# The MLP's Relu and square written to a row in SBUF instead of back into the PSUM bank, in units 0 to 4

## The chip, the cores and the metric

One core of a Trainium2 chip runs the kernel. The metric is the time of one execution on the device in microseconds (us); of several runs the median is taken.

Five engines work side by side, each through its own list of instructions in order: PE (TensorE, matmuls; its weight loads are listed apart as PEld), DVE (VectorE), ACT (ScalarE), POOL (GpSimd) and SP (SyncE, which here only issues DMAs). An engine that meets an instruction whose inputs are not ready waits there, and everything behind it in its list waits too. Matmuls write into PSUM, here in banks of 128 partitions by 512 f32 values; the other engines work on PSUM and on SBUF.

## The reference

Two rounds, each of a long convolution and an MLP, on 2048 tokens (S) of width D = 1024, hidden width F = 3584, all f32:

```python
def _A_ref(q, k, v, shift_k, ssm_k, ssm_D):
    for t in range(ks):                      # ks = 4, causal
        k_shift = k_shift + k_pad[:, t:t + S, :] * shift_k[:, ks - 1 - t][None, None, :]
    kv = k_shift * v
...                                          # long convolution along S by FFT
    y = y + kv * ssm_D[None, None, :]
    return q * y

def _B_ref(x, w1, b1, w2, b2):
    h = jnp.einsum("bsd,df->bsf", x, w1) + b1
    r = jnp.where(h > zero, h, zero)
    h = r * r
    return jnp.einsum("bsf,fd->bsd", h, w2) + b2

x = A_q
x = x + _A_ref(_layernorm(x), A_k, A_v, A_shift_k, A_ssm_k, A_ssm_D)
x = x + _B_ref(_layernorm(x), B_w1, B_b1, B_w2, B_b2)
x = x + _A_ref(_layernorm(x), A_k, A_v, A_shift_k, A_ssm_k, A_ssm_D)
x = x + _B_ref(_layernorm(x), B_w1, B_b1, B_w2, B_b2)
```

The change lies in `h = r * r` of the MLP.

## The kernel before

**Products.** Every f32 operand of a matmul is split into a high half `hi` (a cast to the PE's format fp32r) and a low half `lo = x - hi`. A product is then three matmuls, hi·hi, hi·lo and lo·hi, issued by `mm3` (lines 333 to 336).

**Units.** The MLP runs in eight units, one per layer and block of 512 tokens, in the order of line 35. Units 0 to 4 take the plain path, with which the change deals; units 5, 6 and 7 have a path of their own (`relu_w`, line 1540), in which Relu and square already go to a row in SBUF. Beside the units' matmuls, and woven into them step by step, run the convolution of the blocks to come, the normalization and the additions of results.

**A plain unit** has four chunks of seven hidden tiles of 128. For each hidden tile there are two steps "m1" of 12 matmuls each: they fill one bank [128 x 512] with W1·x. Then come the chunk's 14 steps "m2" (two halves of the output width by seven hidden tiles, 12 matmuls each), which multiply the results, `rh` and `rl`, by W2. The first hidden tile of the next chunk is put between the two halves. Unit 0 is followed by the unit of layer 1 on the same block; its last chunk runs "m2" on half of the tokens at a time, and at its end the first m1 steps of unit 1 are done ahead, some of them in other banks.

**Banks.** An m1 tile takes its bank from `ps1` (line 305), which has two in turn; the four of `ps2` hold the outputs, and two named `pt` belong to the convolution and are passed around by hand with `take` and `give` (lines 314 to 331). Line 1802 picks the bank, and only tiles done ahead on a `pt` bank are returned with `give`. A bank of `ps1` comes free by itself when its last reader has run; the matmul that wants it waits for that.

**Between m1 and m2** stands `relu2` (lines 1483 to 1494). Lines 1813 and 1814 schedule its first part (`k == 0`, on ACT: Relu with bias, square, cast to `rh`) one step after the tile's last m1 step, and its second part (`k == 1`, on DVE: the subtraction that gives `rl`) two steps after it. `lag` is a list of such delayed calls. The instructions then stand in their engines' lists behind whatever was issued before.

**The weights** are streamed from DRAM through a ring of `RAWS = 8` rows in SBUF, `wr`, of 128 x 512 f32 each. `row()` (line 971) takes a row; `drop` (line 978) marks it as read; `room()` (line 968) allows a load when the row eight places back was dropped at least two steps ago. `w_load` (line 982) issues the load on SP up to 8 steps ahead of the weight's use (lines 993, 995, 998), `w_hi` (line 1000) the cast on ACT up to 4 steps ahead (line 1006, into `whl`), `w_lo` (line 1009) the subtraction up to 3 ahead (line 1014, on DVE but for a part of unit 0's last chunk), and with it the row is dropped. `w_advance` (line 1024) calls them at each step. If the ring is full of rows that aren't dropped, `row()` issues the pending casts and subtractions earlier. Some split weights are stored by line 1022 and fetched ready-made later by line 1004, with no row.

**The convolution** issues work on all engines between the steps: line 354 and on for the data (364 and 366 on DVE, 411 the stores), line 428 and on for the filters (482 and 483 on DVE, 492 the stores), line 624 the loads of factors, line 524 the products on POOL, 528 their sums on DVE, 605 the stores of results.

Of the kernel before, what the change touches and what calls it, by code (L numbers as in the profile page):

```python
# [10 lines left out]
F32 = mybir.dt.float32  # L11
F32R = mybir.dt.float32r
AF = mybir.ActivationFunctionType
# [226 lines left out]
def tile_h3_mlp(ctx: ExitStack, tc: tile.TileContext, q, kT, vT, shk, ssmT, ssmD, w1, b1, w2, b2,  # L240
                fwd_t, pro_t, inv_t, sgn_t, out):
    nc = tc.nc
    V, A, G, PE, SY = nc.vector, nc.scalar, nc.gpsimd, nc.tensor, nc.sync
# [85 lines left out]
    def give(*tiles):  # L329
        for o in tiles:  # L330
            held[slot.pop(id(o))[0]] = False
# [639 lines left out]
    def row():  # L971
        while len(ring) >= RAWS and "freed" not in ring[-RAWS]:
            w_hi() if ptr["lo"] == ptr["hi"] else w_lo()
        x = {"t": mw.tile([P, 512], F32, name="wr", bufs=RAWS)}
        ring.append(x)
        return x

    def drop(*xs):
        for x in xs:
            x["freed"] = now[0]  # L980
# [19 lines left out]
    def w_hi():  # L1000
        n = ptr["hi"]
        t = his[n] = mw.tile([P, 2, 512], F32R, name="whl", bufs=6)
        if from_pair(n):
            SY.dma_start(t.bitcast(F32), WD[wsrc[n]])
        else:
            A.copy(t[:, 0], raws[n]["t"])  # L1006
        ptr["hi"] += 1

    def w_lo():
        n = ptr["lo"]  # L1010
        t = wts[n] = his.pop(n)
        if not from_pair(n):
            e = WLO.get(phase[0], "V")
            ENG[e[n % len(e)]].tensor_sub(t[:, 1], raws[n]["t"], t[:, 0].bitcast(F32))  # L1014
            drop(raws.pop(n))
        ptr["lo"] += 1
# [462 lines left out]
    b1t = ml.tile([P, FT], F32, name="b1t", bufs=1)  # L1479
# [1 line left out]
    lag = slag  # L1481

    def relu2(st, k):
        o = st["o"]
        if k == 0:
            A.activation(o, o, AF.Relu, bias=b1t[:, st["f"]:st["f"] + 1])  # L1486
            A.activation(o, o, AF.Square)
            st["hi"] = ml.tile([P, T], F32R, name="rh", bufs=FC + 1)
            A.copy(st["hi"], o)  # L1489
        else:  # L1490
            st["lo"] = ml.tile([P, T], F32R, name="rl", bufs=FC + 1)
            V.tensor_sub(st["lo"], o, st["hi"].bitcast(F32))  # L1492
            if st["give"]:
                give(o)

    def make_t():
        parts = [(p, dq) for p in range(FT // 2) for dq in range(2)]
# [269 lines left out]
    for s, (k, u, c, a, i, tts, w) in enumerate(steps):  # L1767
# [27 lines left out]
        if k == "m1":  # L1795
# [8 lines left out]
            o = rs[c, a]["o"]  # L1804
            for kk in range(4):
                t = slice(kk * P, (kk + 1) * P)
                mm3(o[:, t0:t1], wh[:, t], wl[:, t], xh[:, 4 * i + kk, t0:t1], xl[:, 4 * i + kk, t0:t1],
                    i == 0 and kk == 0, i == 1 and kk == 3)
            if i == 1 and u in WINO:
                for kk in range(4 if rs[c, a]["f"] % 2 else 2):  # L1810
                    lag.at(1 + kk, relu_w, rs[c, a], kk, rp)
            elif i == 1 and tts[-1] == NT - 1:
                lag.at(1, relu2, rs[c, a], 0)
                lag.at(2, relu2, rs[c, a], 1)
        elif k == "w2":
# [6 lines left out]
            hi, lo = rp[i][a]  # L1822
            for n in range(2):
                t = slice(n * P, (n + 1) * P)
# [11 lines left out]
        else:  # L1836
            if i == 0:
                os = {tt: ps2() for tt in tts}
            r = rs[c, i]
            for tt in tts:  # L1840
                t = slice(tt * P, (tt + 1) * P)
# [124 lines left out]
```

## Time and profile before

| | us |
|---|---|
| runs | 2754.60, 2755.72, 2758.86 |
| median | 2755.72 |
| profiled execution, first to last instruction | 2756.1 |
| granted PE clock, mean | 0.992 of full |
| PE busy / idle in it | 2694.2 / 61.9 |
| moved by DMA | 756.88 MB, 275 GB/s |

The profiled execution is one more run of the same program, taken by the hardware's profiler; its own time is its span. The chain of work that ended last is traced back from the last instruction, with shares of the span by engine:

```profile
PE 86%; DVE 6%; DMA 5%; issue 1%; ACT 1%; SPq 1%; POOL 0%; DVEq 0%; ACTq 0%; POOLq 0%
```

An engine's "busy" is the time in which one of its instructions ran; in a wait's row, "p <- DVE rl" is read as: PE's matmul into bank p waited for DVE's instruction that wrote rl. SPq is SP's list of DMA issues.

### The profile page before, as it was taken

How to read it: one execution, taken by the hardware profiler on the slowest of the kernel's cores; microseconds unless marked ns; L12 is line 12 of the kernel's file. 1: busy time of each engine (PE TensorE's matmuls, PEld its weight loads, DVE VectorE, ACT ScalarE, POOL GpSimd, SP SyncE). 2: the span in 40 equal slices, each digit the busy share in tenths (PEclk: the TensorE clock that was granted, in tenths of full speed). 3: DMA queues.
4: the chain of work that ended last, by engine and by line, in shares of the span. 5: the costliest groups of instructions: out<-in, count | busy, mean ns of one | idle time of the engine just before them, and what ended most of it. 6: DMA issues, size and time to landing. Idle time of an engine off the chain costs nothing.

```text
span 2756.1 us, 36563 instructions
## 1 busy us (share of the span) xinstructions
PE 2694.2 (98%) x12601; PEld 2237.7 (81%) x12601; DVE 1935.9 (70%) x3068; ACT 1110.9 (40%) x1937; POOL 826.3 (30%) x531
## 2 busy tenths in 40 slices
PE   7999899899999999999999999999999999999999
PEld 7888787887788888888788888888788788888887
DVE  7878797677787677778676655376787666664555
ACT  4354344433434333342233422244355454444443
POOL 2345564244542645326454265000100010001000
PEclk9999999999999999999999999999999999999999
DMA  8889898589988898788887877688898766676555
GB/s 260 267 298 321 281 311 287 199 302 351 305 294 308 305 330 294 272 303 302 317 286 259 310 270 286 217 290 292 303 308 274 289 229 214 226 275 204 176 164 202
DMA packets 378057, 756.88 MB, mean 275 GB/s; under 512 B 43904, under 2 KB 159248, under 8 KB 377872
## 3 DMA queue, kind: packets, MB, share of 16 engines
q1 hardware_dynamic: 377872, 754.55, 79.8%
q8 instruction: 99, 1.62, 0.2%
q14 instruction: 86, 0.70, 0.1%
HBM read 604.46 MB, written 149.95 MB: 274 GB/s over the span
## 4 chain that ended last, share of the span: by engine, by line
PE 86%; DVE 6%; DMA 5%; issue 1%; ACT 1%; SPq 1%; POOL 0%; DVEq 0%; ACTq 0%; POOLq 0%
PE p L334 26%; PE p L335 26%; PE p L336 26%; PE p L1089 2%; DMA wr<-w 1%; PE pt L336 1%; PE pt L335 1%; PE pt L334 1%; DVE whl L1014 1%; DMA whl<-wd_m 1%; DMA wd_m<-whl 0%; PE pt L594 0%; PE p L788 0%; DVE sm L528 0%; DMA cg<-gd 0%
## 5 line engine op out<-in xcount | busy, mean ns | idle before, releaser
L334 PE MATMUL p<-xh,whl 128*128 128x512 f32 (+1 forms) x1840 | 710.3, 386 | 20.2 <-DVE rl L1492 19.0
L524 POOL TENSOR_TENSOR cp<-cx,cg 128x384 f32<-128x384 f32 (+5 forms) x288 | 534.0, 1867 | 617.7 <-DVE sm L528 397.7
L336 PE MATMUL p<-xh,whl 128*128 128x512 f32 (+1 forms) x1840 | 705.9, 384 | 0.0
L335 PE MATMUL p<-xl,whl 128*128 128x512 f32 (+1 forms) x1840 | 705.5, 383 | 0.1
L1006 ACT CAST whl<-wr 128x512 fp32r<-128x512 f32 x638 | 385.9, 622 | 450.1 <-PE p L336 274.8
L334 PE MATMUL p<-whl,rh 128*128 128x512 f32 x1372 | 547.8, 399 | 1.8 <-DMA whl<-wd_m 1.7
L335 PE MATMUL p<-whl,rh 128*128 128x512 f32 x1372 | 543.0, 396 | 4.9 <-DVE whl L1014 4.9
L1014 DVE TENSOR_TENSOR whl<-wr,whl 128x512 fp32r<-128x512 f32 x624 | 489.4, 805 | 76.9 <-ACT whl L1006 72.1
L336 PE MATMUL p<-whl,rl 128*128 128x512 f32 x1372 | 542.3, 395 | 0.0
L334 PEld LDWEIGHTS p<-xh,whl 128*128 128x128 f32 x1840 | 347.7, 189 | 91.0 <-DVE rl L1492 11.9
L336 PEld LDWEIGHTS p<-xh,whl 128*128 128x128 f32 x1840 | 347.4, 189 | 68.2
L335 PEld LDWEIGHTS p<-xl,whl 128*128 128x128 f32 x1840 | 347.6, 189 | 66.5 <-DVE xl L1402 0.3
L335 PEld LDWEIGHTS p<-whl,rh 128*128 128x128 f32 x1372 | 259.4, 189 | 64.0 <-DVE whl L1014 6.4
L334 PEld LDWEIGHTS p<-whl,rh 128*128 128x128 f32 x1372 | 259.2, 189 | 62.2 <-DMA whl<-wd_m 4.0
L336 PEld LDWEIGHTS p<-whl,rl 128*128 128x128 f32 x1372 | 259.0, 189 | 60.7
L528 DVE TENSOR_REDUCE sm<-cp 128x128 f32<-128x384 f32 (+5 forms) x288 | 249.8, 875 | 13.2 <-POOL cp L524 11.4
L1590 POOL TENSOR_TENSOR acc<-acc,px 128x512 f32<-128x512 f32 x18 | 23.1, 1318 | 770.3 <-DMA px<-b 770.3
L1486 ACT ACTIVATE p<-p,b1t 128x512 f32<-128x512 f32 x138 | 91.7, 664 | 395.6 <-PE p L336 395.4
L1492 DVE TENSOR_TENSOR rl<-p,rh 128x512 fp32r<-128x512 f32 x138 | 94.9, 688 | 221.0 <-ACT rh L1489 220.8
L1554 DVE TENSOR_TENSOR rl<-wr,rh 128x256 fp32r<-128x256 f32 x84 | 51.0, 607 | 207.6 <-ACT rh L1549 207.4
L1613 DVE TENSOR_TENSOR acc<-p,acc 128x512 f32<-128x512 f32 x152 | 101.5, 688 | 90.8 <-PE p L336 90.3
L1546 ACT ACTIVATE wr<-p,b1t 128x512 f32<-128x512 f32 x84 | 58.0, 690 | 188.5 <-PE p L336 184.9
(280 smaller groups left out, 3306.0 us busy)
## 6 DMA issues: line engine op xcount, KB each, us to landing
whl<-wd_m SPq DMA_DIRECT2D x382, 512.0 KB, 5.1
wr<-w SPq DMA_DIRECT2D x494, 256.0 KB, 5.3
wr<-td SPq DMA_DIRECT2D x152, 256.0 KB, 4.2
wd_m<-whl SPq DMA_DIRECT2D x70, 512.0 KB, 6.2
cx<-xd SPq DMA_DIRECT2D x48, 512.0 KB, 5.4
cg<-gd SPq DMA_DIRECT2D x48, 512.0 KB, 6.5
gd<-fg SPq DMA_DIRECT2D x72, 256.0 KB, 6.7
cx<-xd SPq DMA_DIRECT2D x48, 384.0 KB, 6.1
```

Of the source, the lines that this page charges most:

```text
L334: PE.matmul(o, lh, rh, start=start, stop=False)
L335: PE.matmul(o, lh, rl, start=False, stop=False)
L336: PE.matmul(o, ll, rh, start=False, stop=stop)
L524: G.tensor_mul(pr.rearrange("p c i -> p i c"), xt[:, 0:j + 1], gt[:, j::-1])
L528: V.tensor_reduce(sm[:, ty, jj], st["pr"], axis=AX.X, op=OP.add)
L1006: A.copy(t[:, 0], raws[n]["t"])
L1014: ENG[e[n % len(e)]].tensor_sub(t[:, 1], raws[n]["t"], t[:, 0].bitcast(F32))
L1089: PE.matmul(o, lh, r, start=start, stop=stop)
L1486: A.activation(o, o, AF.Relu, bias=b1t[:, st["f"]:st["f"] + 1])
L1492: V.tensor_sub(st["lo"], o, st["hi"].bitcast(F32))
L1546: A.activation(r, st["o"], AF.Relu, bias=b1t[:, st["f"]:st["f"] + 1])
L1613: V.tensor_add(accs[tt][:, d], o, accs[tt][:, d])
```

## The change

The first part of `relu2` takes a row of the ring of weights, writes the Relu from the bank into it, squares the row in place and casts it to `rh`; a bank that has to be given back by hand is given back right behind the Relu. The second part subtracts `rh` from the row, no longer from the bank, and drops the row. What is computed stays the same. In the changed kernel the Relu has line 1487, the square 1490, the cast 1492 and the subtraction 1495.

```diff
@@ -1481,17 +1481,19 @@
     lag = slag
 
     def relu2(st, k):
-        o = st["o"]
         if k == 0:
-            A.activation(o, o, AF.Relu, bias=b1t[:, st["f"]:st["f"] + 1])
-            A.activation(o, o, AF.Square)
+            st["r"] = row()
+            r = st["r"]["t"]
+            A.activation(r, st["o"], AF.Relu, bias=b1t[:, st["f"]:st["f"] + 1])
+            if st["give"]:
+                give(st["o"])
+            A.activation(r, r, AF.Square)
             st["hi"] = ml.tile([P, T], F32R, name="rh", bufs=FC + 1)
-            A.copy(st["hi"], o)
+            A.copy(st["hi"], r)
         else:
             st["lo"] = ml.tile([P, T], F32R, name="rl", bufs=FC + 1)
-            V.tensor_sub(st["lo"], o, st["hi"].bitcast(F32))
-            if st["give"]:
-                give(o)
+            V.tensor_sub(st["lo"], st["r"]["t"], st["hi"].bitcast(F32))
+            drop(st["r"])
 
     def make_t():
         parts = [(p, dq) for p in range(FT // 2) for dq in range(2)]
```

The order in which PE works is unchanged but for the numbers of buffers. On ACT, at the first hidden tile of unit 0 (`p_1135` is its bank, `b1t` the bias, `wr` a row of the ring), there stood before

```order
L1006 CAST whl<-wr 128x512 x2
L1486 ACTIVATE p_1135<-p_1135,b1t 128x512
L1487 ACTIVATE p_1135<-p_1135 128x512
L1489 CAST rh<-p_1135 128x512
L1006 CAST whl<-wr 128x512 x2
```

and now

```order
L1006 CAST whl<-wr 128x512 x2
L1487 ACTIVATE wr<-p_1135,b1t 128x512
L1490 ACTIVATE wr<-wr 128x512
L1492 CAST rh<-wr 128x512
L1006 CAST whl<-wr 128x512 x2
```

The instructions stand in the same places; the bank is now read once, by the Relu, and the row written by it. On DVE, in unit 0 at about 433 to 444 us of the profile, before (`p_4194` is the bank, `fx` and `fg` are tiles of the convolution)

```order
L528 TENSOR_REDUCE sm<-cp 128x128
L364 SCALAR_TENSOR_TENSOR fx<-fx,shkt 128x512 x3
L366 TENSOR_TENSOR fx<-fx 128x512
L482 TENSOR_TENSOR fg<-pt,fg 128x2x2x64
L483 TENSOR_TENSOR fg<-pt,fg 128x2x2x64
L1492 TENSOR_TENSOR rl<-p_4194,rh 128x512
L1014 TENSOR_TENSOR whl<-wr,whl 128x512
```

and now

```order
L528 TENSOR_REDUCE sm<-cp 128x128
L364 SCALAR_TENSOR_TENSOR fx<-fx,shkt 128x512 x3
L366 TENSOR_TENSOR fx<-fx 128x512
L482 TENSOR_TENSOR fg<-pt,fg 128x2x2x64
L483 TENSOR_TENSOR fg<-pt,fg 128x2x2x64
L1495 TENSOR_TENSOR rl<-wr,rh 128x512
L1014 TENSOR_TENSOR whl<-wr,whl 128x512
```

The subtraction keeps its place behind the convolution's work and reads the row instead of the bank. What moves is on SP: with rows taken by the Relus, loads of weights find room later. The following is SP's list in unit 0's last chunk, right behind the three stores of line 492; `wd_m` is the store of a split weight, `yd_102` a result of the convolution, `xd`, `gd`, `kd` and `ssmT` are its data in DRAM, and x2 or x3 stands for so many alike in a row. Before:

```order
L998 DMA wr<-w 128x512
L605 DMA yd_102<-wr 512x1x64
L998 DMA wr<-w 128x512
L624 DMA cx<-xd_73 128x512
L624 DMA cg<-gd_74 128x512
L624 DMA cx<-xd_71 128x512
L624 DMA cg<-gd_75 128x512
L426 DMA fg<-ssmT 128x2x128 x2
L435 DMA fk<-kd_1_86 128x256 x2
L605 DMA yd_102<-wr 512x1x64
L998 DMA wr<-w 128x512
L1022 DMA wd_m_3_0_0_4484<-whl 128x1024
```

Now:

```order
L998 DMA wr<-w 128x512
L605 DMA yd_102<-wr 512x1x64
L624 DMA cx<-xd_73 128x512
L624 DMA cg<-gd_74 128x512
L624 DMA cx<-xd_71 128x512
L624 DMA cg<-gd_75 128x512
L426 DMA fg<-ssmT 128x2x128 x2
L435 DMA fk<-kd_1_86 128x256 x2
L605 DMA yd_102<-wr 512x1x64
L1022 DMA wd_m_3_0_0_4506<-whl 128x1024
L998 DMA wr<-w 128x512 x3
```

Counted by weights, the load that stood right ahead of the stores of line 492 now stands right behind them; the one that stood right behind them now stands behind the first store of line 1022, as do the two that followed it here.

## The prediction

> **What bounds the kernel now.** I read the page's busy table first, then the waits of PE, then windows around those waits, then the timeline of the engine that ended them.
>
> ```profile
> span 2756.1 us, 36563 instructions
> PE 2694.2 (98%) x12601; PEld 2237.7 (81%) x12601; DVE 1935.9 (70%) x3068; ACT 1110.9 (40%) x1937; POOL 826.3 (30%) x531
> ```
>
> PE is busy for 98% of the span: matmuls set the time, and only what PE waits for can be won. The profiled execution's span, 2756.1 us, lies 0.4 us above the median of the runs, 2755.7, so I make the sum against 2755.7. The waits of PE name what is left:
>
> ```profile
> PE p L334 <- DVE rl L1492: 19.0, 6, 5.0
> ...
> PE pt L419 <- DVE fx L366: 6.1, 1, 6.1
> PE p L335 <- DVE whl L1014: 5.2, 2, 4.9
> ```
>
> The columns are us in total, times, longest. The largest entry is the line that the change rewrites: in 6 places the first matmul of a new bank waits until VectorE has subtracted the low half out of the bank before last. These are the six places, with what came after four of them (length, busy time of each engine, then PE's granted clock):
>
> ```profile
> core 0: us, PE busy (x) PEld busy (x) DVE busy (x) ACT busy (x) POOL busy (x), PEclk, DMA share, GB/s
> 332.40:334.10 1.70, 0.14 (x2) 0.09 (x1) 1.70 (x3) 1.55 (x3) 1.70 (x2) 1.00 0.74 245
> 439.40:444.50 5.10, 0.16 (x2) 0.12 (x1) 5.03 (x7) 2.87 (x5) 4.94 (x5) 0.70 0.56 188
> 444.50:451.30 6.80, 6.80 (x26) 5.61 (x27) 5.50 (x11) 0.39 (x1) 2.49 (x3) 0.72 0.47 154
> 624.70:629.70 5.00, 0.03 (x2) 0.02 (x1) 5.00 (x7) 1.83 (x3) 2.50 (x2) 0.95 1.06 366
> 629.70:636.50 6.80, 6.80 (x24) 5.51 (x25) 4.88 (x11) 0.62 (x1) 5.19 (x3) 0.79 1.06 389
> 722.30:726.40 4.10, 0.05 (x1) 0.08 (x1) 4.03 (x5) 2.87 (x5) 2.67 (x3) 0.80 1.03 406
> 726.40:733.20 6.80, 6.80 (x25) 5.65 (x26) 6.25 (x8) 0.00 (x0) 2.90 (x2) 0.62 0.32 115
> 885.70:886.90 1.20, 0.06 (x2) 0.02 (x1) 1.20 (x3) 1.09 (x2) 0.00 (x0) 1.00 1.02 358
> 1314.80:1317.20 2.40, 0.09 (x2) 0.07 (x1) 2.36 (x4) 1.83 (x3) 0.34 (x1) 1.00 0.87 288
> 1317.20:1324.00 6.80, 6.80 (x29) 5.79 (x30) 4.55 (x7) 0.00 (x0) 4.97 (x5) 0.75 1.04 315
> ```
>
> Length less PE's busy time is the wait: 1.56, 4.94, 4.97, 4.05, 1.14 and 2.31, together 18.97 us. Behind four of them the clock is down, so a wait is paid twice. How one comes about, in time:
>
> ```profile
> 432.50 0.78 DVE L1014 TENSOR_TENSOR whl<-wr,whl 128x512 fp32r<-128x512 f32 x1
> 434.07 0.67 ACT L1486 ACTIVATE p<-p,b1t 128x512 f32<-128x512 f32 x1 [2.38 <-PE p L336]
> 438.31 3.56 DVE L364 SCALAR_TENSOR_TENSOR fx<-fx,shkt 128x512 f32<-128x512 f32 x3
> 443.59 0.68 DVE L1492 TENSOR_TENSOR rl<-p,rh 128x512 fp32r<-128x512 f32 x1
> 444.41 0.77 PE L334 MATMUL p<-xh,whl 128*128 128x512 f32 x1 [4.94 <-DVE rl L1492]
> ```
>
> The bank is full and its Relu starts at 434.07; PE wants it back at 439.4, one bank of matmuls later. The Relu is over at 434.74, but the subtraction, queued behind the convolution's work on DVE, runs only at 443.59.
>
> **Removed.** After the change a bank is free when the Relu has read it, at 434.74 in this place. The other five are alike; at 722.3 PE wants the bank whose Relu began 5.5 us before:
>
> ```profile
> 716.77 0.67 ACT L1486 ACTIVATE p<-p,b1t 128x512 f32<-128x512 f32 x1
> ```
>
> The six waits go: 18.97 us. The clock behind them goes too: the matmul at 444.41 took 0.77 and one at full clock (466.54, below) 0.39, so I take the loss as proportional: 6.80 x (0.28 + 0.21 + 0.38 + 0.25) = 7.6 us. Sum 26.6 us, of which 8.4 in unit 0 (1.56 + 4.94 + 1.90) and 18.2 in units 1 to 3.
>
> In "TensorE: Matmul & The Clock Gate", section "What's actually happening", the Trainium skill lets the clock drop only after an idle window of about 3.4 us. By that rule the wait of 2.31 us would have cost no clock, and the sum would be 24.9; the row 1317.20:1324.00 with 0.75 speaks against it.
>
> **Kept by units 1 to 3: 18.2 us.** What is late next there is DVE itself, still behind at the moment the wait goes. It catches up and then idles for work of PE's, within 6 to 16 us:
>
> ```profile
> 737.90 0.69 DVE L1492 TENSOR_TENSOR rl<-p,rh 128x512 fp32r<-128x512 f32 x1 [5.25 <-ACT rh L1489]
> 1327.91 0.69 DVE L1492 TENSOR_TENSOR rl<-p,rh 128x512 fp32r<-128x512 f32 x1 [6.12 <-ACT rh L1489]
> ```
>
> PE comes 6.6 and 4.0 us earlier at these two places; the pauses of 5.25 and 6.12 us take that up but for a little at the first, and what still lies late on DVE, the subtraction, no longer holds a bank.
>
> **Added on ACT and DVE.** The Relu now writes SBUF, the square, the cast and the subtraction read it. The last three units do just that already, at lines 1546 and 1547:
>
> ```profile
> L1486 ACT ACTIVATE p<-p,b1t x138: 656/664/687, 140.8 to 1826.5; 128x512 f32<-128x512 f32 x138
> L1546 ACT ACTIVATE wr<-p,b1t x84: 674/691/693, 1874.5 to 2711.1; 128x512 f32<-128x512 f32 x84
> L1487 ACT ACTIVATE p<-p x138: 582/583/583, 141.5 to 1827.2; 128x512 f32<-128x512 f32 x138
> L1547 ACT ACTIVATE wr<-wr x84: 632/635/637, 1875.2 to 2711.8; 128x512 f32<-128x512 f32 x84
> L1006 ACT CAST whl<-wr x638: 599/622/648, 138.8 to 2739.0; 128x512 fp32r<-128x512 f32 x160
> L1492 DVE TENSOR_TENSOR rl<-p,rh x138: 674/692/693, 142.7 to 1828.4; 128x512 fp32r<-128x512 f32 x138
> L1014 DVE TENSOR_TENSOR whl<-wr,whl x624: 674/686/2897, 143.8 to 2744.7; 128x512 fp32r<-128x512 f32 x156
> ```
>
> ACT: 140 x (27 + 52 + some 35 for the cast) = 16 us on an engine busy 40%: hidden. DVE: the subtraction out of PSUM never took over 693 ns; the same operation between SBUF tiles has nearly the same median but goes up to 2897. Three windows of line 1014 alone give its mean by stage:
>
> ```profile
> 120.00:520.00 400.00, 96.98 (x107) 14.66 (x11) 0.97 0.89 299
> 520.00:800.00 280.00, 53.61 (x50) 4.33 (x3) 0.97 0.85 294
> 800.00:1860.00 1060.00, 126.75 (x142) 0.00 (x0) 1.00 0.83 290
> ```
>
> 906, 1072 and 893 ns, against 688: 28 x 0.22 + 28 x 0.38 + 84 x 0.21 = 34 us of DVE over the five units, at least 0 (same median) and at most 140 x 2.2 = 309. It costs PE only where DVE ends PE's wait, in some three places of unit 0 and 1 (366 and 1014 in the waits above): I take 1.0 us, between 0 and 3 x 2.2 = 6.6.
>
> **Added on the ring of rows.** The Relu takes one of 8 rows, whose last reader is mostly line 1014 of the step before. In the place above that ended at 433.28, before the Relu's 434.07, so no new wait for ACT; 0. But each row that a Relu holds is one that no weight can be loaded into, and SP's order moves. In unit 0's last chunk, as the order piece shows, one load moves from behind the stores of line 492 to behind the store of line 1022:
>
> ```profile
> 447.16 1.44 SPq L492 DMA_DIRECT2D gd<-fg  x3
> 448.69 0.45 SPq L998 DMA_DIRECT2D wr<-w  x1
> ...
> 457.53 0.38 SPq L1022 DMA_DIRECT2D wd_m<-whl  x1
> ...
> wr<-w SPq DMA_DIRECT2D x494, 256.0 KB, 5.3
> ...
> 462.30 2.49 DVE L1014 TENSOR_TENSOR whl<-wr,whl 128x512 fp32r<-128x512 f32 x4
> ...
> 466.54 0.39 PE L334 MATMUL p<-whl,rh 128*128 128x512 f32 x1
> ```
>
> The load of 448.69 belongs to the second of the four subtractions from 462.30, and to the matmul at 466.54: 3.0 us of slack. In the new order it is issued at 455.0 to 457.9 (two loads that stood before it now follow, and the two stores of line 605 wait less; I take 457.9, the end of the store at 457.53, as the late bound and 2.9 less as the early one); the stores at 447.16 stay, being held by DVE. Landing 5.3 later, cast 0.62, subtraction 0.69: ready at 461.6 to 464.5. PE, 8.4 us earlier, wants it at 458.1. A wait of 3.5 to 6.4 replaces the one removed at 439.4; I take 3.8, the early end, as SP has little left to wait for, and 1.5 for the clock behind it (1.4 to 2.6 in the windows above): 5.3 us given back.
>
> **Sum.** 26.6 - 5.3 - 1.0 = 20.3 us; 2755.7 - 20.3 = 2735.4. I say 2735.
>
> **The rivals.**
> 1. *Nothing is given back*: loads run early enough (SP pulled forward by PE). All 26.6: 2729. For it: SP's waits there may be PE's in disguise. Against: the hold of line 492 until 447.16 is DVE's. Chance 0.20.
> 2. *Unit 0 loses more*: weights late by the new order in its other chunks too, where a cast follows its load by one step in place of three. Two such places with 3.8 + 1.5 cost 10.6 more: 2746. Chance 0.17.
> 3. *The port decides*: each of the 28 subtractions in unit 1 and the 28 in unit 0 that meets a POOL operation stretches, DVE lags more, and the waits named at lines 419 and 335 grow. Two thirds of 56 at 0.3 us make 11 us, and two more stretches of low clock at 2.6 another 5: 2755.7 - 26.6 + 5.3 + 16 = 2751. For it: maxima of 2897. Against: DVE has pauses. Chance 0.08. The Trainium skill has this rule in "SBUF — State Buffer", section "Who interferes with whom": VectorE with two SBUF inputs contends with a GpSimd instruction that reads SBUF, with one it does not; the 693 and 2897 above agree.
> 4. *Slower: PE starves for weights in unit 0.* The ring is short by a row all through the unit, so at each chunk's turn a weight comes late. Six places at 3.8 + 2.6 make 38 us against 26.6 gained: 2755.7 + 12 = 2768. It decides from the point where loads lead their casts by less than the landing of 5.3 us. Against: weights there have some 3 us and more of slack. Chance 0.07.
>
> That the change doesn't do what it says can be left out: in the order of the changed program the Relu is the bank's only reader.
>
> **How the numbers follow.** Forecast 0.48, rivals 0.20, 0.17, 0.08, 0.07. The forecast's own range is 2731 to 2740. The range takes in rivals 1 and 2, with 3 and 4 us beyond for the unknown sizes, and stops before 3 and 4, 0.15 left out: 2726 to 2750. A measurement here tells 0.2%, 5.5 us, from no change. Faster: 0.48 + 0.20 + 0.17 = 0.85; within 0.2%: 0.08; slower: 0.07.
>
> **What would show it.** The entry of PE waiting on the subtraction gone, with no wait for the Relu in its place; clock 1.00 behind 624, 722 and 1314; a new wait of PE on line 1014 or a load around 455 to 465, in rival 1 none; the new subtraction's mean 0.9 to 1.1 us; DVE's busy time up by some 30. Wrong would be waits on `whl` all over unit 0 (rival 4), or line 419 waiting longer (rival 3).

## The result and the profile after

| | before | changed | ratio (95%) |
|---|---|---|---|
| first comparison, median us | 2757.29 | 2742.02 | 0.9942 (0.9928 to 0.9957) |
| changed kernel measured again | 2761.22 | 2741.10 | 0.9938 (0.9924 to 0.9952) |
| profiled execution, span us | 2756.1 | 2740.4 | |

The change makes the kernel faster by 0.6%: 15.3 us by the medians of the first comparison, 20.1 by those of the second, 15.7 by the two profiles. The ratios are estimated from all runs and are not quotients of the medians; they make it 16 and 17 us. Forecast were 20.3 (2735, range 2726 to 2750). The two head lines of the changed kernel's page:

```profile
span 2740.4 us, 36599 instructions
PE 2690.7 (98%) x12601; PEld 2234.9 (82%) x12601; DVE 1986.9 (73%) x3068; ACT 1124.4 (41%) x1937; POOL 842.5 (31%) x531
```

VectorE does the same 3068 instructions and is busy 51 us longer. The waits of PE, in us (total, times, longest):

```profile
...
PE p L334 <- DMA whl<-wd_m: 8.3, 11, 2.5
PE pt L419 <- DVE fx L366: 7.2, 2, 5.3
...
PE p L335 <- DVE whl L1014: 3.5, 3, 2.9
PE pt L594 <- ACT whl L1006: 1.9, 1, 1.9
```

The 19.0 us of the bank's subtraction are gone, and no wait for the Relu stands in their place. New are a wait at line 594 and longer ones for stored weights. The stretches that had half a clock behind the waits at 624, 722 and 1314 lie at these times now, by windows (length, busy times, granted clock, DMA):

```profile
core 0: us, PE busy (x) PEld busy (x) DVE busy (x) ACT busy (x) POOL busy (x), PEclk, DMA share, GB/s
622.40:629.20 6.80, 6.80 (x31) 5.63 (x30) 6.80 (x8) 3.02 (x5) 3.93 (x2) 1.00 1.00 291
717.50:724.30 6.80, 6.80 (x37) 5.87 (x36) 6.73 (x7) 3.59 (x6) 4.55 (x4) 1.00 0.99 380
1302.10:1308.90 6.80, 6.80 (x37) 5.87 (x36) 6.73 (x10) 1.95 (x3) 2.99 (x3) 1.00 0.95 333
```

PE's order is the same in both programs, so its n-th matmul can be set beside its n-th. This table was worked out from the starts of single matmuls in the profiles: how much later (+) or earlier (-) than before they start, at each place just ahead of and behind what happens there. The third column is the second profile of the changed kernel; the last two are runs told of below, one with a buffer of its own for the Relu and one with the change on six tiles alone.

```
us in the profile of before   changed  again  own buffer  six tiles
 256 (all of it before 138)     +0.7    +4.5     0.0        +0.1
 330                            +3.2    +5.7    +2.1        -1.1
 341 (wait at 332 gone)         +1.3    +3.8    +0.3        -2.9
 449 (wait at 439 gone)         -5.7    -2.5    -6.0        -9.9
 563 (rest of unit 0)           -1.4    +3.5     0.0        -9.1
 636 (wait at 624 gone)         -8.1    -3.1    -6.7       -15.7
 718                            -4.0    -2.2    -4.5       -10.1
 737 (wait at 722 gone)        -10.7    -8.9   -11.2       -16.3
 896 (wait at 885 gone)        -12.1   -10.3   -12.6       -17.7
1327 (wait at 1314 gone)       -16.1   -14.4   -16.7       -22.0
2752 (end)                     -15.7   -15.2   -15.6       -22.3
```

The six places bring 1.9 + 7.0 + 6.7 + 6.7 + 1.4 + 4.1 = 27.8 us in the first profile and the same in the second. The rest, 12.1 us, is lost between them: 0.7 at the start, 2.5 from 256 to 330, 4.3 from 449 to 563, 4.1 from 636 to 718, the rest in small steps. The second profile loses 12.6, but not in the same places: 4.5 at the start, 1.2 from 256 to 330, 6.0 from 449 to 563, only 0.9 from 636 to 718.

What is lost at the start is not the change's: all of it stands already at 138 us, and the first Relu that the change rewrites comes at 140.8. Counted from 138 on the change gains 16.4 us in the first profile and 19.7 in the second. Nor is the profile of before a fixed mark. In the runs with the ring alone and with units 1 to 4 alone, told of below, unit 0 waits for its banks as before the change; counted the same way they lie 2.6 and 0.8 us later at 563. So a us or two at a single place may be chance.

### The profile page after: what moved, and what is told of

Same layout as the page of the kernel before. It is cut to its first block, busy times and chain, and to the rows that moved or that the text cites. A ratio compares the mean times of both kernels' runs of the same rounds, so it can differ in the third digit from the quotient of the medians.

```text
span 2740.4 us, 36599 instructions
## 1 busy us (share of the span) xinstructions
PE 2690.7 (98%) x12601; PEld 2234.9 (82%) x12601; DVE 1986.9 (73%) x3068; ACT 1124.4 (41%) x1937; POOL 842.5 (31%) x531
## 4 chain that ended last, share of the span: by engine, by line
PE 87%; DMA 6%; DVE 4%; POOL 1%; issue 1%; SPq 1%; ACT 0%; DVEq 0%; ACTq 0%; POOLq 0%
PE p L334 27%; PE p L335 26%; PE p L336 26%; DMA whl<-wd_m 2%; PE p L1089 2%; DMA wr<-w 1%; PE pt L335 1%; PE pt L336 1%; PE pt L334 1%; DMA wd_m<-whl 1%; POOL acc L1592 0%; DMA fx<-kT 0%; DMA px<-x 0%; PE pt L390 0%; PE p L788 0%
## 5 line engine op out<-in xcount | busy, mean ns | idle before, releaser
L524 POOL TENSOR_TENSOR cp<-cx,cg 128x384 f32<-128x384 f32 (+5 forms) x288 | 541.2, 1892 | 585.9 <-DVE sm L528 376.4
L1014 DVE TENSOR_TENSOR whl<-wr,whl 128x512 fp32r<-128x512 f32 x624 | 500.1, 821 | 77.6 <-ACT whl L1006 68.9
L1495 DVE TENSOR_TENSOR rl<-wr,rh 128x512 fp32r<-128x512 f32 x140 | 139.4, 997 | 188.7 <-ACT rh L1492 188.6
L1487 ACT ACTIVATE wr<-p,b1t 128x512 f32<-128x512 f32 x138 | 95.2, 690 | 375.1 <-PE p L336 374.2
L1548 ACT ACTIVATE wr<-p,b1t 128x512 f32<-128x512 f32 x84 | 57.9, 689 | 187.3 <-PE p L336 186.8
```

Source lines behind the costliest of these rows:

```text
L524: G.tensor_mul(pr.rearrange("p c i -> p i c"), xt[:, 0:j + 1], gt[:, j::-1])
L1487: A.activation(r, st["o"], AF.Relu, bias=b1t[:, st["f"]:st["f"] + 1])
L1495: V.tensor_sub(st["lo"], st["r"]["t"], st["hi"].bitcast(F32))
L1548: A.activation(r, st["o"], AF.Relu, bias=b1t[:, st["f"]:st["f"] + 1])
```

## The experiments

Three questions were open: whether the bank's earlier release is the whole gain, what gives 8 to 11 us back (the late load of the forecast, the stretched VectorE, or something else), and whether a smaller edit keeps more. Times are medians. The kernel before was measured anew beside each of three groups of runs: 2760.74 us beside the first four, 2761.22 beside the next four, 2760.28 beside the last three.

**A buffer of its own.** The Relu takes no row of the ring, so the loads of weights stand in SP's list as before the change, but for two that still come behind the first store of line 1022 in unit 0's last chunk.

```diff
-            st["r"] = row()
+            own = st.get("u", 0) < 4 and st["f"] < 3 * FC + 4
+            st["r"] = {"t": ml.tile([P, T], F32, name="yt", bufs=2)} if own else row()
```

> The change, but in units 0 to 3 the Relu of all tiles up to the fourth of the last chunk goes to a buffer of its own (two that stand unused there) and takes no row of the ring; the loads of weights then stand in SP's list as before the change. Ours: the ring costs only what the late load at 465 costs, 0.7 to 1.3 us; the waits for the convolution's bank (1.9 us at 443) and for stored weights (1.5 at 478, 2.5 at 635) stay, and the new subtraction still takes 0.95 to 1.05 us. Time 1 to 2 us under the changed kernel's 2742, about 2740. Rival (the late load was what took the rest of the gain, as forecast with 5.3 us): the waits between 440 and 485 go, 2735 to 2737.

2741.07 us, ratio 0.9933 (0.9918 to 0.9947): the changed kernel's time. Two waits from its list:

```profile
PE p L335 <- DVE whl L1014: 4.9, 5, 3.3
...
PE pt L594 <- DVE fg L483: 2.6, 1, 2.6
```

The forecast's late load is back in its old place, and nothing waits for it; unit 0's end still gives back 6.0 us (table, 449 to 563). That load is not what the gain goes to. The stretch is there as well: the 100 subtractions that read the own buffers take 1068 ns in the mean.

**The bank held.** As changed, but the subtraction names a column of the bank that it does not use.

```diff
-            V.tensor_sub(st["lo"], st["r"]["t"], st["hi"].bitcast(F32))
+            V.scalar_tensor_tensor(st["lo"], st["r"]["t"], st["o"][:, 0:1], st["hi"].bitcast(F32),
+                                   op0=OP.bypass, op1=OP.subtract)
```

> The change, but the subtraction also names one column of the PSUM bank as an operand that it does not use, so that the bank is free only when VectorE has run, as before the change; rows, ring and the order of loads are the change's. Ours (the gain is the bank's earlier release and nothing else): the six waits of PE on the subtraction come back with 19 us or more, and with a stretched VectorE the time is 2757 to 2770. Rival (the gain comes from the order of the loads or from the PSUM ports being freer): 2742 to 2747, no such wait.

2767.52 us, ratio 1.0029 (1.0017 to 1.0041). Its longest entry among PE's waits:

```profile
PE p L334 <- DVE rl L1493: 21.9, 8, 5.2
```

The bank's waits are back with 21.9 us, and the whole gain is gone. What is left against the kernel before, 0.17 to 0.41% or 4.7 to 11.3 us, is the price of everything else in the change (and of 0.06 us more for each of these instructions): VectorE is busy 1990.9 us here, 55 more than before. Of it 2.9 us are the bank's waits themselves, 21.9 us for 19.0, which the changed kernel does not have; so this is more than the changed kernel pays.

**The ring alone.** The kernel before, with a row taken at each Relu and dropped behind the subtraction, but not used.

```diff
             A.activation(o, o, AF.Square)
+            st["r"] = row()
...
             V.tensor_sub(st["lo"], o, st["hi"].bitcast(F32))
+            drop(st["r"])
```

> The kernel before, with a row of the ring taken at each Relu and dropped behind the subtraction but neither written nor read: only the order of the loads is the change's. Ours: within 3 us of before, 2755 to 2760. Rival (late loads): 4 to 6 us more than before, 2761 to 2764, with PE waiting on line 1014 or on the load between 455 and 490.

2759.92 us, ratio 1.0008 (0.9996 to 1.0020): no cost that can be told from none, and no new wait at the loads, though SP's list in unit 0 is that of the changed kernel. But PE comes no earlier here, and by the prediction's own figures (the weight ready by 464.5 at the latest, PE there at 466.5) no wait was to be expected. The run clears the ring only for a PE that still waits for its banks. Of what the run before is charged, it leaves the stretch of VectorE as the likeliest cause; shown alone it is not.

**Units 1 to 4 alone.** Unit 0 keeps the old `relu2`.

> The change in units 1 to 4 alone; unit 0 as before the change. Ours: from the two traces, matched matmul by matmul, unit 0 gains only 2 us net (8.3 us at 332 and 439, given back at 260, 443, 465 and 478), so the time is 2743 to 2746. Rival (unit 0 keeps some 8 us): 2750. Other rival (unit 0 loses on the whole): under 2741.

2743.48 us, ratio 0.9947 (0.9933 to 0.9962). As matched: unit 0 gives most of what its two places gain back, and nearly all of the gain is made in units 1 to 3. From 138 us on this profile gains 16.7 us, against 16.4 and 19.7 of the changed kernel.

**The changed kernel again.**

> The changed kernel once more, to see which of its waits come back in a second profile. Ours: 0.994 of before; the waits at 295 and 488 and the one for the convolution's bank at 443 come back within 1 us, since VectorE's order sets them; the one for a stored weight at 635 (2.5 us, only 0.9 and 0.5 with the two kernels that differ from this one in unit 0) does not, being a matter of how late one transfer lands. Rival: 635 comes back with 2 us or more, as a part of the price of the change.

Its time stands in the first table. Two of its waits:

```profile
PE p L334 <- ACT whl L1006: 1.9, 1, 1.9
PE pt L594 <- DVE fg L483: 1.9, 1, 1.9
```

The waits at 295 (6.05 for 5.34), 443 (1.87 for 1.93) and 488 (3.25 for 2.93) came back, the one at 635 did not. So some 3 us of what the first profile gives back (4.1 from 636 to 718, where this one has 0.9) are how one transfer happened to land (the wait of 2.5 us in its list). In its place this profile has the first wait shown here, at 466: the late load of the forecast, with 1.9 us and half a clock behind it (in the matched starts 3.9 us).

**The subtraction on GpSimd.** `V.tensor_sub` becomes `G.tensor_sub` in the changed kernel's second part.

> The change, with the subtraction that reads the row on GpSimd in place of VectorE (units 0 to 4). VectorE is rid of 139 us, GpSimd gets 140 x 1.3 = 182 us. If VectorE's stretched subtractions are what costs PE at 260, 295, 443 and 553 (together some 10 us in the changed kernel): those waits shrink by half or more, 2735 to 2738. Rival (GpSimd's products and the sums behind them come later, and VectorE's other two-input operations are stretched in place of this one): 2742 to 2750, with the waits for the convolution's tiles as long as before.

2770.07 us, ratio 1.0042 (1.0027 to 1.0058): slower than before, and by more than the rival said. What SP waits for in the changed kernel, and then here:

```profile
SPq L624 <- POOL cp L524: 57.2, 28, 5.4
```

```profile
SPq L624 <- POOL cp L524: 228.0, 63, 11.2
```

And PE's longest entry here, with one that is 0.2 us at most in the other profiles:

```profile
PE p L334 <- DMA whl<-wd_m: 16.5, 16, 4.6
...
PE p L788 <- ACT wr L731: 5.8, 5, 2.4
```

GpSimd's products come later, the loads of line 624 wait in SP's list for the buffers that these products read, and the loads of stored weights stand behind them in the same list. The wait for the convolution's bank, 1.9 us in the changed kernel, is 3.8 here. So this run does not tell what a VectorE rid of the subtraction would bring.

**A later subtraction.** The kernel with a buffer of its own, `lag.at(2, relu2, ..., 1)` made `lag.at(4, ...)`.

> As the run with a buffer of its own, with the subtraction two steps later still: nothing waits for it before its chunk's second product, so the convolution's work stands ahead of it on VectorE. If the subtractions in front of the convolution's work are what makes its bank late at 443 and its tiles at 260 and 295: 2 to 4 us less, 2737 to 2739. Rival (the backlog is the convolution's own work, so the order changes nothing): 2740 to 2743, the wait at 443 still 1.9 to 2.7 us.

2741.52 us, ratio 0.9941 (0.9925 to 0.9956); the wait at 443 is 1.4 us, 1.2 less than with the own buffer alone and under the rival's 1.9. So the order on VectorE is a part of that wait, but it changes the time by nothing that can be measured; the rest of the backlog there is the convolution's own.

**The subtraction twice.** The same instruction a second time.

> The change, with each of the 140 subtractions done twice: 139 us more on VectorE, with the same banks, rows and loads. If VectorE's time has a price (3 us for the 44 us by which the change stretched the subtractions): 6 to 12 us over the changed kernel, 2748 to 2754, in longer waits for the convolution's tiles and for line 1014. Rival (VectorE's time is free now that it holds no bank of the MLP): within 2 us, 2740 to 2744.

2778.02 us, ratio 1.0068 (1.0053 to 1.0083): 36.9 us over the changed kernel measured beside it, three times the upper end of what was expected. PE's waits:

```profile
PE p L335 <- DVE whl L1014: 11.5, 7, 4.2
PE pt L419 <- DVE fx L366: 9.9, 4, 5.9
PE p L334 <- DMA whl<-wd_m: 6.6, 8, 2.6
PE pt L594 <- DVE fg L483: 5.3, 1, 5.3
```

VectorE is busy 2137.6 us, 151 more, and each us of it costs 0.24. That VectorE holds no bank of the MLP any more does not make its time free: it still makes weights and the convolution's tiles.

**Every third subtraction left out.**

```diff
+            if st["f"] % 3 == 2:
+                st["lo"] = st["hi"]
```

> The change, with the subtraction of every third hidden tile left out (f = 2, 5, 8, ...: 45 of 140; the high half stands in for the low one there, so that part of the result is left out). VectorE is rid of some 45 us, as much as the stretch by the change cost it. Ours (VectorE's time has a price of 0.15 to 0.26 us of time for each us, by the runs with the bank held and with the subtraction done twice): 6 to 11 us under the changed kernel, 2730 to 2735, ratio 0.990 to 0.992. Rival (only more of it costs, less brings nothing, since what is left of PE's waits is set by other things): 2739 to 2742, ratio 0.994.

2737.86 us, ratio 0.9925 (0.9912 to 0.9939), VectorE busy 1952.4 us. Between the two: 3.2 us under the changed kernel's 2741.10, for 34 us less of VectorE, 0.09 each. But the two were not measured beside each other, and the intervals of their ratios overlap: a gain is not shown, and the interval takes in the upper end of my range (0.992) as well as the rival's 0.994. What less of VectorE's time is worth stays open.

**Six tiles, and twelve.** A counter picks the tiles that go to a row; the others keep the old `relu2`.

> The change for six of the 140 tiles alone, those whose bank PE waited for before (the 16th, 25th, 37th, 45th, 57th and 93rd); all others as before the change. No stretch of VectorE to speak of, and the loads stand almost as before. Ours (the change gains 26 us and gives 8 to 10 back by the stretch and the ring): the six waits go, no other bank is waited for by more than 1 us, and the time is 3 to 8 us under the changed kernel, 2733 to 2738, ratio 0.9905 to 0.9925. Rival (the backlog on VectorE simply stops PE at the next bank, the one behind each of the six): new waits on the subtraction of 2 us and more, 2742 to 2748, ratio 0.994 to 0.997.

> The same for twelve tiles: the six and the one behind each. Ours: as with six or up to 2 us better, ratio 0.990 to 0.9925. Rival (next bank): waits on the subtraction gone here though not with six, and 3 us or more better than with six.

Six: 2739.76 us, ratio 0.9927 (0.9914 to 0.9939). Twelve: 2738.19, ratio 0.9921 (0.9909 to 0.9934). Of the six's waits:

```profile
PE pt L419 <- DVE fx L366: 4.6, 1, 4.6
PE p L334 <- DVE rl L1507: 3.8, 2, 3.6
...
PE p L335 <- DVE whl L1014: 3.2, 4, 2.1
PE pt L594 <- DVE fg L483: 2.3, 1, 2.3
```

Six tiles of 140 carry the whole gain. Both theories have a part: unit 0's end gives back only 0.8 us net (table, 449 to 563), for a reason told below, but at 621 PE stops at the next bank, which still waits for its subtraction, for 3.6 us (5.6 with the clock). With twelve that wait is gone, and one of 1.4 us stands at the bank after it. These are the lowest medians of kernels that compute all of the result, 1.3 to 3.8 us under the changed kernel's; the intervals overlap, so that they beat it is not shown.

## Why the prediction was right, and where it was not

The time lies in the range and the direction is right. Of the 20.3 us forecast the first comparison has 15.3 by its medians and 16 by its ratio, the second 20.1 and 17; the two profiles have 16.4 and 19.7 from 138 us on.

**The six waits go: right.** 26.6 us were forecast for them with the clock, 27.8 were measured by matched matmuls, in both profiles. The run with the bank held shows that nothing else in the change gains. That a wait of 2.31 us costs clock was also right: the place at 1314 brought 4.1 us, more than the wait itself.

**Units 1 to 3 keep what they gain: nearly.** From 737 to the end 5.2 us were forecast (the waits at 885 and 1314 with the clock), 5.0 and 6.3 came. Of the 4.1 us lost behind 636 in one profile the other has 0.9.

**Given back in unit 0's last chunk, 5.3 us by a late load: right in size, not in its cause.** 4.3 and 6.0 us were given back from 449 to 563, but that load is not what decides it, since 6.0 are given back with the load in its old place too. That the size fits is luck: the 5.3 us were worked out for one late load, and several waits and the clock make up what was found. What PE met first was the next thing that hangs on the same backlog of VectorE, one bank of the convolution. The timeline of the changed kernel there:

```profile
439.89 3.59 DVE L364 SCALAR_TENSOR_TENSOR fx<-fx,shkt 128x512 f32<-128x512 f32 x3
443.52 1.10 DVE L366 TENSOR_TENSOR fx<-fx 128x512 f32<-128x512 f32 x1
444.54 0.41 DVE L482 TENSOR_TENSOR fg<-pt,fg 128x256 f32<-128x256 f32 x1
444.87 0.41 DVE L483 TENSOR_TENSOR fg<-pt,fg 128x256 f32<-128x256 f32 x1
445.20 0.83 DVE L1495 TENSOR_TENSOR rl<-wr,rh 128x512 fp32r<-128x512 f32 x1
445.43 1.78 PE L594 MATMUL pt<-sm,yh 128*128 128x128 f32 x8 [1.93 <-ACT whl L1006]
```

Line 594 writes a `pt` bank that lines 482 and 483 have to read first; they end at 445.28, and a cast on ACT that ended 0.1 us later is what the row names. The other profiles shown here name line 483. Before, the wait for the MLP's bank covered this one. I had asked what is late next on SP and not what is late next on VectorE, although VectorE's order piece has lines 482 and 483 standing right ahead of the subtraction. Behind it PE met stored weights (1.5 us at 478 in the first profile, 1.5 at 485 in the second), and only the old wait for line 1014 at 488 grew shorter, from 4.9 to 2.9 and 3.3 us. The late load itself came as forecast:

```profile
458.80 2.02 SPq L998 DMA_DIRECT2D wr<-w  x3
...
464.24 1.98 ACT L1006 CAST whl<-wr 128x512 fp32r<-128x512 f32 x3 [3.91 <-DMA wr<-w]
464.89 2.06 DVE L1014 TENSOR_TENSOR whl<-wr,whl 128x512 fp32r<-128x512 f32 x3 [3.24 <-ACT whl L1006]
464.91 0.50 PE L334 MATMUL p<-whl,rh 128*128 128x512 f32 x1 [0.17 <-ACT whl L1006]
```

It was issued at 458.80, 0.9 us behind the late bound, and cast from 464.24; but PE, held up at line 594, came as late, and lost 1.0 us here, 0.2 in the wait for the cast and the rest for the subtraction. In the second profile it lost 3.9.

**1.0 us for the stretched subtraction: probably too low, by how much stays open.** The page of the changed kernel (busy us, mean ns):

```profile
L1014 DVE TENSOR_TENSOR whl<-wr,whl 128x512 fp32r<-128x512 f32 x624 | 500.1, 821 | 77.6 <-ACT whl L1006 68.9
...
L1495 DVE TENSOR_TENSOR rl<-wr,rh 128x512 fp32r<-128x512 f32 x140 | 139.4, 997 | 188.7 <-ACT rh L1492 188.6
```

The mean of 997 ns was forecast (0.9 to 1.1 us); VectorE's busy time, up by 51 us, was put at some 30. It is a matter of GpSimd: 65 of the 140 subtractions overlap with one of its instructions and take 1353 ns in the mean, 75 do not and take 687; before, with the bank as input, 59 overlapped and took 688, no more than the other 81 (counted from the starts and ends in the two traces). The Trainium skill's rule that I made the third rival ("SBUF — State Buffer", section "Who interferes with whom") agrees with these counts. But I let the stretch cost PE something only where VectorE ended a wait before, and it delays everything that VectorE does. What speaks for a higher price: from 256 to 330 the changed kernel loses 2.5 and 1.2 us, with a new wait at 260 in the first profile (1.9 us, line 419), while six tiles lose -1.1 and twelve 0.4; the run with the bank held costs 4.7 to 11.3 us, but a part of that is its own; and six and twelve tiles have the lower medians, though by no more than the intervals allow. From these I estimate 1 to 4 us. No run isolates it.

Unit 0's end, where six tiles give back 0.8 us, twelve 2.1 and the changed kernel 4.3 and 6.0, does not show the stretch. PE waits there as long without it: its waits of 0.4 us and more from 440 to 563, without the one of 3.8 us at line 1701 that all have (line 1722 with six and twelve), add up to 8.1 us with six tiles and 8.1 with twelve, to 7.2 and 9.3 in the two profiles of the changed kernel. The wait at line 594 is 2.3 us with six tiles, where none of the 140 subtractions takes over 0.82 us. What differs is the clock behind the waits: 10.2 us at half clock there in either profile of the changed kernel, 3.4 with twelve tiles, none with six. How little of that is the edit's shows behind the wait at line 1701: it is 3.8 us in all four profiles, and 6.8, 3.4, 3.4 and no us at half clock follow it (changed, again, twelve, six). The last section has the reason. The profiled execution with six tiles is also the fastest of its five, 3.7 us under their median.

**ACT is hidden, the Relu waits for no row: right.** ACT is busy 13.5 us longer (forecast 16), and only 0.9 us of its Relus' idle time was ended by a row's last reader in the first profile, 3.8 by VectorE in the second.

**The rivals.** Nothing given back (2729, 0.990 of before): excluded by both ratios. Unit 0 loses more (2746): its end loses about what was forecast, and from 256 to 330 it loses 1.2 to 2.5 us, not 10.6. The port decides: the mechanism is there, but the price of 16 us that I gave it is not; line 419's waits, the sign that I named, are 7.2 and 6.7 us, against 6.1 before. Slower for want of weights: no; the kernel is faster, and its waits for weights come nowhere near six places at 6.4 us.

## What to carry to other kernels

When an engine's wait for a backlogged engine is removed, look next at what else the waiting engine needs from the same backlog: that is what it meets, a few us later. A buffer that a slow reader holds can be freed by copying only where the wait is; here 6 of 140 tiles carry the gain, and that the other copies cost something is likely but not shown. VectorE's time has a price although PE is the bound and VectorE is busy only 73%: here 0.24 us for each us added by doing the subtractions twice. And a profile is one execution: set a second one of the same kernel beside it before a loss of a us or two is given a cause.

## What the runs showed of the hardware that was not expected

The clock was granted in stretches of 3.413 us on a fixed grid, and a wait cost clock by how it fell on that grid, not by its length alone. Every half-clock stretch of a profile begins at a whole multiple of 3.413 us from the others, within 0.002. Windows on the grid for a wait of 2.31 us of the kernel before (length, busy times, granted clock, DMA; the length less PE's busy time is its idle time):

```profile
1311.84:1315.25 3.41, 2.98 (x14) 2.13 (x12) 3.38 (x3) 0.39 (x1) 2.85 (x1) 1.00 0.93 312
1315.25:1318.67 3.42, 1.54 (x7) 1.26 (x8) 3.38 (x5) 1.44 (x3) 0.00 (x0) 1.00 0.92 296
1318.67:1322.08 3.41, 3.41 (x12) 2.85 (x11) 3.08 (x6) 0.00 (x0) 3.13 (x2) 0.50 1.04 350
1322.08:1325.49 3.41, 3.41 (x20) 2.98 (x20) 0.00 (x0) 0.00 (x0) 3.33 (x4) 1.00 1.07 332
```

The wait of 1.93 us at line 594 in the changed kernel:

```profile
442.31:445.73 3.42, 1.49 (x9) 0.98 (x8) 3.35 (x6) 1.75 (x3) 3.34 (x4) 1.00 0.71 257
445.73:449.14 3.41, 3.41 (x14) 2.93 (x13) 3.38 (x7) 0.38 (x1) 2.86 (x2) 0.50 0.00 0
449.14:452.55 3.41, 3.41 (x22) 3.06 (x21) 3.41 (x7) 1.55 (x3) 1.00 (x1) 1.00 0.73 223
```

The wait of 2.65 us at the same line in the kernel with a buffer of its own, which falls across two windows:

```profile
440.66:444.07 3.41, 2.49 (x11) 1.72 (x10) 3.31 (x4) 2.79 (x5) 3.25 (x3) 1.00 0.80 243
444.07:447.49 3.42, 1.69 (x12) 1.58 (x13) 3.42 (x5) 0.00 (x0) 3.42 (x3) 1.00 0.25 96
447.49:450.90 3.41, 3.25 (x19) 2.70 (x18) 3.38 (x8) 0.38 (x1) 1.50 (x2) 1.00 0.11 34
```

A window with 1.88 or 1.93 us of idle PE is followed by one at half clock, one with 0.92 and then 1.73 is not: the longer wait is the cheaper one. Over the thirteen profiles from 115 us on, windows at full clock that idled 2.0 us and more were followed by half clock and those under 1.6 were not, with both outcomes in between: four windows of 1.90 to 1.93 us with six tiles kept the full clock, two of them those on which the 3.8 us at line 1722 fell half and half. The Trainium skill ("TensorE: Matmul & The Clock Gate", "What's actually happening") has a free-running window of this length, and the grid agrees; that the clock drops only after an idle window does not, since about half of one is enough. A part of what is given back, of the differences between two profiles of one kernel, and of what six tiles seem to save in unit 0's end is this.
